# Attention scores of a head pair in two groups of 512 columns instead of three of 384, 384 and 288

## The chip, the cores and the metric

The kernel runs on one core of a Trainium2 chip. The core has a matrix engine (TensorE, "PE" in the profile, with its weight loads as "PEld"), a vector engine (VectorE, "DVE"), a scalar engine (ScalarE, "ACT"), a general engine (GpSimd, "POOL"), and a sync engine (SyncE, "SP") whose queue issues most of the transfers. TensorE writes its results into PSUM, a small memory of eight banks of 512 f32 columns by 128 partitions; the other operands lie in SBUF. The metric is the device time of one execution in microseconds, lower is better.

## What is computed

For 8 batches and 8 heads there are 512 local tokens and 32 global ones, head size 64. Global queries see all keys. A local query sees the 32 global keys and the local keys at most 32 positions away. The attention's output is the input of a dense layer with a softplus between two products.

```python
s_g = scale * np.matmul(q_g, k_all.transpose(0, 1, 3, 2))
out_g = np.matmul(sm(s_g), v_all)
mask = np.abs(pos[:, None] - pos[None, :]) <= window      # window = 32
s_ll = np.where(mask, scale * np.matmul(q_l, k_l.transpose(0, 1, 3, 2)), -1000000000.0)
s_lg = scale * np.matmul(q_l, k_g.transpose(0, 1, 3, 2))
out_l = np.matmul(sm(np.concatenate([s_lg, s_ll], axis=-1)), v_all)
x = np.concatenate([out_g, out_l], axis=2)    # to 4608 rows of 512
h = x @ w_in                                  # 512 x 2048
out = (np.maximum(h, 0.0) + np.log1p(np.exp(-np.abs(h)))) @ w_out
```

## The kernel before

The 64 heads are handled as 32 pairs m, four to a batch; the two heads of a pair lie in partitions 0 to 63 and 64 to 127, so that their products with 64 contraction rows can run side by side on TensorE.

**The local stage.** Pairs 0 to 5 (`M0 = 6`) are computed first, in another form (`scores0`, `turn0`, `values0` and their global counterparts), as 15 steps of a software pipeline with index k; `stage(k, f)` runs phase f of step k. Their exponentials sit in tiles of tags "x", "wo8" and "wo9" (`exps0`). The first 16 weight tiles are split into high and low halves in between.

**The MoE.** For each batch b and each of 16 slices f of the hidden size, `hpart` makes 12 products into tile h, `act` runs softplus (three operations on ACT, one on DVE that writes e, a cast gh on ACT, a difference gl on POOL), and `opart` makes 12 products into the four output tiles o. The operands are f32 numbers split into two reduced-precision halves, three products for each. An o run stands two h runs and one o run or more behind the h run it uses (`behind = 2`), and at a batch's start less (`behind = 1`). A ninth block handles the global tokens. Batch 0 runs while the rest of the weights are still being split (`weights`), batch b needs the pairs 4b to 4b+3 (`split_x`).

**The pieces.** Pairs 6 to 31 are cut into pieces with a position each, and the loop over the MoE's items issues a piece when the position is reached: pair m has its three groups of scores at 12m, 12m+4 and 12m+8, its totals at 12m+18 (`TOT`), its values and normalising at 12m+22 (`VAL`). A batch is 48 positions long. Pieces below `START = 77` are issued inside the local stage, at k = n-2: the first two groups of pair 6.

**A pair.** Global keys are repeated in front of each of six chunks of 96 local keys, so a chunk has 128 keys, held in the partitions. A group p of scores holds two chunks: the queries that can see them, 192 columns a chunk (96 for the last). `scores` (from line 296) makes a product for each chunk and head, f32, into one tile of two PSUM banks, a head to a bank. For pairs 6 and 7 (`m < MPE`) TensorE also adds the mask by a product with the identity, and ACT copies the result; for later pairs DVE adds the mask while it copies (L325). Then DVE takes block maxima over 32 columns with a transposing reduction (L326). After the third group `maxima` folds these (POOL copies L339, small DVE operations L342 to L352), and `probs`, for each group, spreads the maxima (DVE transposes, L360), subtracts them on POOL (L365 to L368), takes the exponential on ACT (L369) and reduces sums on DVE (L374). `totals` folds the sums, `values` multiplies by V, two heads in the two column halves, into a tile of two PSUM banks, and `normalise` scales and writes x.

**Queues and buffers.** The order on TensorE is the order of the program (`mm`); on the other engines a scheduler orders the work, with some orders fixed by hand (`keep`, `after`). In the local stage and early batch 0 scores use the PSUM tiles "oA" and "oB"; with the first o run these banks are given to the output tiles (`output_banks`), and scores and values then share one tile "a" of two banks. The tiles of scores s are four buffers of 2x384 and two of 2x288, the spread maxima mb two of 2x288. The three raw tiles of a pair (queries and keys of a group) are loaded by SP, each right after the group of the pair before that used its buffer.

Of the kernel before, what the change touches and what calls it, by code (L numbers as in the profile page):

```python
# [8 lines left out]
F32 = mybir.dt.float32  # L9
F32R = mybir.dt.float32r  # L10
BF16 = mybir.dt.bfloat16
I32 = mybir.dt.int32
AF = mybir.ActivationFunctionType
ALU = mybir.AluOpType
# [5 lines left out]
P = 128  # L20
NEG = -8.0e9
LOW = -3.0e38
KW = 96
NPC = 3
QW = (288, 288, 192)
KWID = (256, 256, 256)
EW = (0, 544, 1088)
OUT = (0, 512, 736)
NF = DFF // P

M0 = 6
MPE = 8
VAL = 22
TOT = 18
STEP = 3
GW = 75
W_AHEAD = 13
W_PRE = 16
START = 77
RATE = 3  # L40
A_LO = 8
A_UP = 5
# [7 lines left out]
def windows(ap2d, start, stride, count, width):  # L50
    base = ap2d[:, start:start + width]
    return bass.AP(base.tensor, base.offset, [list(base.ap[0]), [stride, count], [1, width]])
# [3 lines left out]
def moe_over_global_local_attention(  # L56
# [11 lines left out]
    nc = tc.nc  # L68
    PSUM = bass.MemoryType.PSUM
    const = ctx.enter_context(tc.tile_pool(name="const", bufs=1))  # L70
    pl = ctx.enter_context(tc.tile_pool(name="pl", bufs=2))
    ps_h = ctx.enter_context(tc.tile_pool(name="ps_h", bufs=2, space=PSUM))
    ps_a = ctx.enter_context(tc.tile_pool(name="ps_a", bufs=1, space=PSUM))
# [3 lines left out]
    ps_s = first_scores.__enter__()  # L77
# [4 lines left out]


    identf = pl.tile([P, P], F32, tag="e", name="identf", bufs=2)
    mask = const.tile([P, 384], BF16, name="mask")
    mask5 = const.tile([P, 96], BF16, name="mask5")
    ident = const.tile([P, P], BF16, name="ident")

    mask0 = pl.tile([P, 2, 2, 224], BF16, tag="rb", name="mask0", bufs=1)
# [2 lines left out]
    for o, w, base, sign in ((32, 32, 0, 1), (64, 32, -96, -1), (96, 128, 32, 1), (96, 128, 32, -1)):  # L92
        r = mask0[:, 0, 1, o:o + w]
# [5 lines left out]
    make_identity(nc, identf)  # L99

    def key_masks():
        nc.vector.memset(mask, 0.0)
        nc.vector.memset(mask5, 0.0)
        for m, o, w, x0, rows in ((mask, 0, 160, 0, P), (mask, 192, 64, 0, P), (mask, 288, 96, 64, P), (mask5, 0, 64, 0, 64)):
            r = m[0:rows, o:o + w]
            nc.gpsimd.affine_select(r, r, pattern=[[1, w]], compare_op=ALU.is_ge, fill=NEG, base=32 + x0, channel_multiplier=-1)
            nc.gpsimd.affine_select(r, r, pattern=[[-1, w]], compare_op=ALU.is_ge, fill=NEG, base=32 - x0, channel_multiplier=1)
        nc.vector.memset(mask[0:32], 0.0)
        for o in (0, 128, 160, 192, 256, 352):
            nc.vector.memset(mask[0:32, o:o + 32], NEG)  # L110

        nc.vector.memset(mask5[0:32], 0.0)
        nc.vector.memset(mask5[0:32, 0:32], NEG)

        nc.vector.memset(mask5[64:128], NEG)

    order = {}

# [7 lines left out]
    def mm(*a, **k):  # L126
        order["pe"] = after(nc.tensor.matmul(*a, **k), "pe").ins  # L127
# [3 lines left out]
    st = {}  # L131
# [28 lines left out]
    count0 = []  # L160

    def exps0(shape, name):
        count0.append(name)
        tag = ("x", "wo8", "x", "wo9")[len(count0) % 4]
        return pl.tile(shape, F32, tag=tag, name=f"e0_{name}", bufs=2 if tag == "x" else 1)

    def soft0(name, ps, views, outs):

# [116 lines left out]
    def load(m, p):  # L285
        w = QW[p] + KWID[p]
        raw = pl.tile([P, 544], F32, tag="raw", name=f"raw{m}_{p}", bufs=3)
        order["load"] = nc.sync.dma_start(out=raw[:, :w], in_=qk[m - M0, :, EW[p]:EW[p] + w]).ins
        st["raw", m, p] = raw
# [3 lines left out]
        nc.sync.dma_start(out=t.rearrange("p h c d -> p (h c d)"), in_=v[m - M0])  # L293
        st["v", m] = t

    def scores(m, p):
        raw = st.pop(("raw", m, p))
        q = QW[p]
        if "o" not in banks:
            ps = ps_s.tile([P, 2, 512], F32, tag=("oA", "oB")[(3 * m + p) % 2], name=f"s_ps{m}_{p}")  # L300
        else:
            ps = ps_a.tile([P, 2, 512], F32, tag="a", name=f"s_ps{m}_{p}")
        parts = ((0, 0, 192), (192, 96, 192 if p < 2 else 96))
        pe_mask = m < MPE
        masks = (mask[:, 0:192], mask[:, 192:384] if p < 2 else mask5)
        for i, (o, qs, w) in enumerate(parts):
            ks = q + 128 * i
            for h in range(2):
                r = slice(64 * h, 64 * h + 64)
                mm(ps[:, h, o:o + w], lhsT=raw[r, ks:ks + P], rhs=raw[r, qs:qs + w],  # L310
                   start=True, stop=not pe_mask, skip_group_check=True)
            for h in range(2 if pe_mask else 0):
                mm(ps[:, h, o:o + w], lhsT=ident, rhs=masks[i], start=False, stop=True, skip_group_check=True)
        if p == 0:
            st["mt", m] = pl.tile([P, 348], F32, tag="mt", name=f"mt{m}", bufs=2)
            nc.gpsimd.memset(windows(st["mt", m], 0, 36, 3, 3), LOW)
        mt = st["mt", m]
        nb = 12 if p < 2 else 9
        s = pl.tile([P, 2, 32 * nb], F32, tag="s" if p < 2 else "s2", name=f"s{m}_{p}", bufs=4 if p < 2 else 2)
        if pe_mask:  # L320
            nc.scalar.copy(s, ps[:, :, 0:32 * nb])  # L321
        else:
            for o, mk in ((0, mask[:, 0:384]),) if p < 2 else ((0, mask[:, 0:192]), (192, mask5)):
                w = mk.shape[1]
                nc.vector.tensor_tensor(s[:, :, o:o + w], ps[:, :, o:o + w], mk.unsqueeze(1).to_broadcast([P, 2, w]), op=ALU.add)  # L325
        order["scores"] = nc.vector.tensor_reduce(windows(mt, 3 + 12 * p, 36, 2, nb), s.rearrange("p h (b k) -> p h b k", k=32),  # L326
                                axis=AX.X, op=ALU.max, apply_transpose=True).ins
        st["s", m, p] = s

    def grid(t, start, *dims):  # L330
        base = t[0:32, start:start + 1]
# [21 lines left out]
        order["maxima"] = i  # L353
        st["e", m] = e

    def probs(m, p):
        s, e = st["s", m, p], st["e", m]
        k = QW[p] // 32
        mb = pl.tile([P, 2, 288], F32, tag="mb", name=f"mb{m}_{p}", bufs=2)
        nc.vector.transpose(mb[:, :, :QW[p]].rearrange("p h (s k) -> p h s k", k=32),  # L360
                            windows(e, 7 * p, 21, 2, k).unsqueeze(3).to_broadcast([P, 2, k, 32]))
        for h in range(2):
            if p < 2:
                sw = s[:, h].rearrange("p (c w) -> p c w", w=192)
                nc.gpsimd.tensor_tensor(sw, sw, windows(mb[:, h], 0, 96, 2, 192), op=ALU.subtract)  # L365
        if p == 2:
            nc.gpsimd.tensor_tensor(s[:, :, 0:192], s[:, :, 0:192], mb[:, :, 0:192], op=ALU.subtract)
            nc.gpsimd.tensor_tensor(s[:, :, 192:288], s[:, :, 192:288], mb[:, :, 96:192], op=ALU.subtract)  # L368
        nc.scalar.activation(s, s, AF.Exp, scale=0.125)  # L369
        if p == 0:  # L370
            st["zt", m] = pl.tile([P, 348], F32, tag="zt", name=f"zt{m}", bufs=2)
            nc.gpsimd.memset(windows(st["zt", m], 0, 36, 3, 3), 0.0)
        nb = 12 if p < 2 else 9
        nc.vector.tensor_reduce(windows(st["zt", m], 3 + 12 * p, 36, 2, nb), s.rearrange("p h (b k) -> p h b k", k=32),  # L374
                                axis=AX.X, op=ALU.add, apply_transpose=True)

    def totals(m):
# [9 lines left out]
    def values(m):  # L387

        vt = st["v", m]
        ps = st["vs", m] = ps_a.tile([P, 2, 512], F32, tag="a", name=f"v_ps{m}")  # L390
        flat = ps.rearrange("p a q -> p (a q)")
        for p in range(NPC):
            s = st.pop(("s", m, p))
            for i, (o, qs, w) in enumerate(((0, 0, 192), (192, 96, 192 if p < 2 else 96))):
                c = OUT[p] + qs
                for h in range(2):
                    mm(flat[64 * h:64 * h + 64, c:c + w], lhsT=vt[:, h, 2 * p + i], rhs=s[:, h, o:o + w],
                       start=p < 2 and i == 0, stop=True, skip_group_check=True)

    SEG = ((lambda t: t[:, 0:128].unsqueeze(1), 0, 1, 128), (lambda t: windows(t, 160, 224, 2, 192), 128, 2, 192))  # L400

# [14 lines left out]
    def pieces():  # L416
        def piece(*fs):
            def go():
                for f in fs:
                    f()  # L420
            return go
        ps = []
        for m in range(M0, M):
            for p in range(NPC):
                fs = [lambda m=m, p=p: scores(m, p)]
                if m + 1 < M:
                    fs.append(lambda m=m, p=p: load(m + 1, p))
                if p == 2:
                    fs.append(lambda m=m: maxima(m))
                    fs += [lambda m=m, q=q: probs(m, q) for q in range(NPC)]  # L430
                ps.append((12 * m + 4 * p, piece(*fs)))
            ps.append((12 * m + TOT, lambda m=m: totals(m)))
            fs = [lambda m=m: values(m), lambda m=m: normalise(m)]
            if m + 2 < M:
                fs.append(lambda m=m: load_v(m + 2))
            ps.append((12 * m + VAL, piece(*fs)))
        ps.sort(key=lambda t: t[0])
        return ps
# [168 lines left out]
    i = order_w.index(("wi", NF - 1))  # L607
# [33 lines left out]
    n = len(steps)  # L641
# [6 lines left out]
    for k in range(-2, n + 2):  # L648
# [9 lines left out]
        if held:  # L658
            r = bits_w(*held)
# [91 lines left out]
```

## Time and profile before

| | |
|---|---|
| median of 3 runs | 1005.15 us (1004.91 to 1005.45) |
| profiled execution, own time | 1005.01 us |
| its span, first to last instruction | 1003.2 us |
| mean granted TensorE clock | 0.987 |
| share of the chain that ended last | TensorE 79%, DVE 1%, all others under 1% |

The profile shows one execution. Its busy shares are averages over stages with different limits, so the stages are read one by one. Ends of matmuls are modelled and overlap their successors, so TensorE's pace is read from start to start. An f32 product appears as two weight loads and two matmuls. All matmuls carry the line of the helper `mm` (L127) and are told apart by tile: h and o for the MoE, s_ps for scores, v_ps for values of pairs 6 to 31, s, s0g, t, t0g, o0g for the local stage.

### The profile page before, as it was taken

How to read it: one execution, taken by the hardware profiler on the slowest of the kernel's cores; microseconds unless marked ns; L12 is line 12 of the kernel's file. 1: busy time of each engine (PE TensorE's matmuls, PEld its weight loads, DVE VectorE, ACT ScalarE, POOL GpSimd, SP SyncE). 2: the span in 40 equal slices, each digit the busy share in tenths (PEclk: the TensorE clock that was granted, in tenths of full speed). 3: DMA queues.
4: the chain of work that ended last, by engine and by line, in shares of the span. 5: the costliest groups of instructions: out<-in, count | busy, mean ns of one | idle time of the engine just before them, and what ended most of it. 6: DMA issues, size and time to landing. Idle time of an engine off the chain costs nothing.

```text
span 1003.2 us, 14264 instructions
## 1 busy us (share of the span) xinstructions
PE 966.0 (96%) x5151; PEld 755.1 (75%) x5151; DVE 645.8 (64%) x1348; ACT 517.5 (52%) x918; POOL 446.1 (44%) x603
## 2 busy tenths in 40 slices
PE   6798989899999999999999999999999999999996
PEld 4576767677777777777777777777777778888895
DVE  6885979856678766776667677776677665211210
ACT  5787656544445544454454444554445445444452
POOL 5664776524444444453345444444435344222221
PEclk9999989989999999999999999999999999999998
DMA  9824322211112111121112111211112100100000
GB/s 354 310 74 144 112 83 60 58 63 48 40 49 90 49 37 48 49 85 43 47 34 90 40 49 49 70 58 49 48 39 89 47 2 16 50 1 1 22 22 21
DMA packets 34302, 66.19 MB, mean 66 GB/s; under 512 B 7608, under 2 KB 11448, under 8 KB 34232
## 3 DMA queue, kind: packets, MB, share of 16 engines
q1 hardware_dynamic: 33416, 65.19, 20.4%
q8 instruction: 40, 0.66, 0.3%
q14 instruction: 30, 0.25, 0.1%
q10 hardware_dynamic: 816, 0.10, 0.1%
HBM read 55.84 MB, written 9.44 MB: 65 GB/s over the span
## 4 chain that ended last, share of the span: by engine, by line
PE 79%; DVE 1%; POOL 0%; issue 0%; ACT 0%; DVEq 0%; POOLq 0%
PE o L127 35%; PE h L127 34%; PE s_ps L127 5%; PE v_ps L127 5%; DVE xl L454 1%; DVE zt L374 0%; POOL wo L499 0%; DVE mb L360 0%; POOL gl L548 0%; DVE wbitswo L490 0%; DVE e L544 0%; ACT ot L566 0%; DVE wlastwo L493 0%; DVE mt L352 0%; DVE mt L342 0%
## 5 line engine op out<-in xcount | busy, mean ns | idle before, releaser
L127 PE MATMUL o<-wo,gh 128*128 128x512 f32 x1088 | 347.5, 400 | 6.2 <-ACT gh L547 4.9
L127 PE MATMUL h<-xh,wi 128*128 128x512 f32 (+1 forms) x1152 | 351.1, 388 | 1.2 <-DVE e L544 0.7
L548 POOL TENSOR_TENSOR gl<-e,gh 128x512 fp32r<-128x512 f32 x136 | 177.8, 1307 | 333.2 <-ACT gh L547 271.1
L127 PEld LDWEIGHTS h<-xh,wi 128*128 128x128 f32 x1152 | 210.3, 190 | 51.4 <-issue 5.6
L127 PEld LDWEIGHTS o<-wo,gh 128*128 128x128 f32 x1088 | 200.9, 189 | 58.3 <-ACT gh L547 5.8
L544 DVE SCALAR_TENSOR_TENSOR e<-h,e 128x512 f32<-128x512 f32 x136 | 93.0, 684 | 234.4 <-ACT e L543 213.9
L127 PE MATMUL h<-xl,wi 128*128 128x512 f32 (+1 forms) x576 | 220.5, 383 | 0.0
L127 PE MATMUL o<-wo,gl 128*128 128x512 f32 x544 | 216.2, 397 | 2.5 <-POOL gl L548 2.5
L541 ACT ACTIVATE e<-h 128x512 f32<-128x512 f32 x136 | 81.3, 598 | 232.2 <-PE h L127 232.2
L547 ACT CAST gh<-e 128x512 fp32r<-128x512 f32 x136 | 84.3, 620 | 112.6 <-DVE e L544 112.6
L365 POOL TENSOR_TENSOR s<-s,mb 128x384 f32<-128x384 f32 x104 | 107.0, 1060 | 51.1 <-DVE mb L360 51.1
L127 PEld LDWEIGHTS h<-xl,wi 128*128 128x128 f32 x576 | 109.0, 189 | 22.7
L127 PEld LDWEIGHTS o<-wo,gl 128*128 128x128 f32 x544 | 102.9, 189 | 27.1 <-POOL gl L548 3.3
L543 ACT ACTIVATE e<-e,one 128x512 f32<-128x512 f32 x136 | 98.4, 723 | 4.2
L542 ACT ACTIVATE e<-e 128x512 f32<-128x512 f32 x136 | 85.7, 630 | 3.4
L325 DVE TENSOR_TENSOR s<-s_ps,mask 128x768 f32<-128x768 f32 (+1 forms) x96 | 64.7, 695 | 29.4 <-PE s_ps L127 29.4
L369 ACT ACTIVATE s<-s 128x768 f32<-128x768 f32 (+1 forms) x78 | 61.7, 790 | 37.1 <-POOL s L365 34.7
L374 DVE TRANSPOSE_TENSOR_REDUCE zt<-s 128x24 f32<-128x768 f32 (+1 forms) x78 | 69.9, 902 | 6.3 <-ACT s L369 4.7
L326 DVE TRANSPOSE_TENSOR_REDUCE mt<-s 128x24 f32<-128x768 f32 (+1 forms) x78 | 69.3, 888 | 5.8 <-ACT s L321 5.1
L127 PEld LDWEIGHTS s_ps<-raw 64*128 64x128 f32 x624 | 48.7, 186 | 29.6 <-issue 22.1
L127 PE MATMUL s_ps<-raw 64*128 64x192 f32 (+1 forms) x624 | 70.1, 340 | 0.7 <-ACT e_g L174 0.7
L127 PEld LDWEIGHTS v_ps<-s,v 128*64 128x64 f32 x624 | 42.5, 137 | 14.3 <-issue 9.0
(134 smaller groups left out, 881.9 us busy)
## 6 DMA issues: line engine op xcount, KB each, us to landing
raw<-in_qk SPq DMA_DIRECT2D x52, 272.0 KB, 2.7
v<-in_v SPq DMA_DIRECT2D x26, 384.0 KB, 3.1
out<-ot SPq DMA_DIRECT2D x34, 256.0 KB, 2.1
wiraw<-in_w_in SPq DMA_DIRECT2D x16, 512.0 KB, 9.1
woraw<-in_w_out SPq DMA_DIRECT2D x16, 512.0 KB, 8.6
raw<-in_qk SPq DMA_DIRECT2D x26, 224.0 KB, 2.5
v<-in_v SPq DMA_DIRECT2D x6, 512.0 KB, 6.0
raw<-in_qk SPq DMA_DIRECT2D x6, 416.0 KB, 7.8
```

What stands on the lines that cost most here:

```text
L127: order["pe"] = after(nc.tensor.matmul(*a, **k), "pe").ins
L325: nc.vector.tensor_tensor(s[:, :, o:o + w], ps[:, :, o:o + w], mk.unsqueeze(1).to_broadcast([P, 2, w]), op=ALU.add)
L326: order["scores"] = nc.vector.tensor_reduce(windows(mt, 3 + 12 * p, 36, 2, nb), s.rearrange("p h (b k) -> p h b k", k=32), axis=AX.X, op=A ...
L365: nc.gpsimd.tensor_tensor(sw, sw, windows(mb[:, h], 0, 96, 2, 192), op=ALU.subtract)
L369: nc.scalar.activation(s, s, AF.Exp, scale=0.125)
L374: nc.vector.tensor_reduce(windows(st["zt", m], 3 + 12 * p, 36, 2, nb), s.rearrange("p h (b k) -> p h b k", k=32), axis=AX.X, op=ALU.add, a ...
L541: nc.scalar.activation(e, ph, AF.Abs)
L542: nc.scalar.activation(e, e, AF.Exp, scale=-1.0)
L543: nc.scalar.activation(e, e, AF.Ln, bias=one)
L544: nc.vector.scalar_tensor_tensor(e, ph, 0.0, e, op0=ALU.max, op1=ALU.add)
L547: nc.scalar.copy(gh, e)
L548: nc.gpsimd.tensor_tensor(gl, e, gh.bitcast(F32), op=ALU.subtract)
```

## The change

A pair's scores, 1056 columns a head before, become 1024 in one order of columns, cut into two groups of 512, a full PSUM bank for each head. Seven products a head take the place of six: the first chunk's product is 160 wide instead of 192 (32 columns of padding are left out), and the third chunk's is made in two parts, 160 columns in the first group and 32 in the second. One mask of 1024 columns takes the place of two masks; for pairs 6 and 7 its product comes first, 512 columns at once, and the scores are accumulated on it. Pairs from 8 on have one mask add a group. One tile of scores s of 2x1024 holds a pair (two buffers). Maxima, exponentials and sums go by the two groups. The spread maxima take four transposes instead of three, into tiles of 2x416, and the subtractions five operations instead of six. `values` has still six products a head, read from the new column order, the first 160 wide. The groups stand at 12m and 12m+6, `TOT` is 17, `VAL` 21 and `START` 80: both groups of pair 6 come before the MoE. The raw tiles are loaded one after the first group and two after the second. The exponentials of the local stage use the tag "s".

```diff
-OUT = (0, 512, 736)
+CHUNKS = ((0, 0, 32, 160), (1, 160, 96, 192), (2, 352, 0, 160), (2, 512, 160, 32), (3, 544, 96, 192), (4, 736, 0, 192), (5, 928, 96, 96))
+VALUES = ((0, 0, 32, 160), (1, 160, 96, 192), (2, 352, 512, 192), (3, 544, 608, 192), (4, 736, 736, 192), (5, 928, 832, 96))
-VAL = 22
-TOT = 18
+VAL = 21
+TOT = 17
-START = 77
+START = 80
...
-    mask = const.tile([P, 384], BF16, name="mask")
-    mask5 = const.tile([P, 96], BF16, name="mask5")
+    mask = const.tile([P, 1024], BF16, name="mask")
...
+        for o, q, w in ((0, 384, 160), (160, 544, 192), (736, 352, 192)):
+            nc.gpsimd.tensor_copy(mask[:, o:o + w], mask[:, q:q + w])
...
-        tag = ("x", "wo8", "x", "wo9")[len(count0) % 4]
+        tag = ("s", "wo8", "s", "wo9")[len(count0) % 4]
...
-    def scores(m, p):
+    def scores(m, g):
...
+        cut = slice(512 * g, 512 * g + 512)
+        for h in range(2 if pe_mask else 0):
+            mm(ps[:, h], lhsT=ident, rhs=mask[:, cut], start=True, stop=False, skip_group_check=True)
+        for c, o, qs, w in CHUNKS:
+            if not cut.start <= o < cut.stop:
+                continue
+            raw, ks, o = st["raw", m, c // 2], QW[c // 2] + 128 * (c % 2), o - cut.start
             for h in range(2):
                 r = slice(64 * h, 64 * h + 64)
                 mm(ps[:, h, o:o + w], lhsT=raw[r, ks:ks + P], rhs=raw[r, qs:qs + w],
-                   start=True, stop=not pe_mask, skip_group_check=True)
-            for h in range(2 if pe_mask else 0):
-                mm(ps[:, h, o:o + w], lhsT=ident, rhs=masks[i], start=False, stop=True, skip_group_check=True)
+                   start=not pe_mask, stop=True, skip_group_check=True)
...
+            st["s", m] = pl.tile([P, 2, 1024], F32, tag="s", name=f"s{m}", bufs=2)
+        s = st["s", m][:, :, cut]
         if pe_mask:
-            nc.scalar.copy(s, ps[:, :, 0:32 * nb])
+            nc.scalar.copy(s, ps)
         else:
+            nc.vector.tensor_tensor(s, ps, mask[:, cut].unsqueeze(1).to_broadcast([P, 2, 512]), op=ALU.add)
...
+    def probs(m, g):
+        s, e = st["s", m], st["e", m]
+        mb = pl.tile([P, 2, 416], F32, tag="mb", name=f"mb{m}_{g}", bufs=2)
+        for o, k, n in (((0, 1, 8), (256, 7, 5)), ((0, 10, 6), (192, 14, 6)))[g]:
+            nc.vector.transpose(mb[:, :, o:o + 32 * n].rearrange("p h (s k) -> p h s k", k=32),
+                                windows(e, k, 21, 2, n).unsqueeze(3).to_broadcast([P, 2, n, 32]))
+        for o, q, w in (((0, 0, 160), (160, 64, 352)), ((512, 64, 32), (544, 0, 384), (928, 288, 96)))[g]:
+            nc.gpsimd.tensor_tensor(s[:, :, o:o + w], s[:, :, o:o + w], mb[:, :, q:q + w], op=ALU.subtract)
+        s = s[:, :, 512 * g:512 * g + 512]
         nc.scalar.activation(s, s, AF.Exp, scale=0.125)
...
+        for k, o, c, w in VALUES:
+            for h in range(2):
+                mm(flat[64 * h:64 * h + 64, c:c + w], lhsT=vt[:, h, k], rhs=s[:, h, o:o + w],
+                   start=k % 2 == 0 and k < 4, stop=True, skip_group_check=True)
...
-            for p in range(NPC):
-                fs = [lambda m=m, p=p: scores(m, p)]
+            for g in range(2):
+                fs = [lambda m=m, g=g: scores(m, g)]
                 if m + 1 < M:
-                    fs.append(lambda m=m, p=p: load(m + 1, p))
+                    fs += [lambda m=m, p=p: load(m + 1, p) for p in ((0,), (1, 2))[g]]
...
-                ps.append((12 * m + 4 * p, piece(*fs)))
+                ps.append((12 * m + 6 * g, piece(*fs)))
```

## What I expected, and why

> **What bounds the kernel now.** I read four views in this order: the page's busy table, the chain of work that ended last, the waits of TensorE, and the windows by stage. The page first:
>
> ```profile
> span 1003.2 us, 14264 instructions
> PE 966.0 (96%) x5151; PEld 755.1 (75%) x5151; DVE 645.8 (64%) x1348; ACT 517.5 (52%) x918; POOL 446.1 (44%) x603
> ```
>
> TensorE is busy nearly throughout, but busy time of pipelined matmuls overlaps, so the chain has to confirm it. Here is the chain over one stretch of the middle; columns are start, length, engine, tile, instructions.
>
> ```profile
> 448.75 0.85 PE s_ps L127 x8
> 449.60 1.59 PE h L127 x6
> 451.19 2.80 PE o L127 x12
> ...
> 466.19 0.72 PE s_ps L127 x8
> 466.90 2.99 PE h L127 x12
> 469.90 1.94 PE v_ps L127 x24
> 471.84 2.96 PE o L127 x12
> ```
>
> Everything here is TensorE. An undisturbed run of 12 MoE matmuls takes 2.80 us; the run after an attention block takes 2.96 to 2.99, so each block costs about 0.17 behind it besides its own length. Now the waits of TensorE from 120 to 205 us (total us, times, longest):
>
> ```profile
> PE o L127 <- ACT gh L547: 4.9, 2, 3.3
> PE o L127 <- POOL gl L548: 2.5, 2, 1.8
> ```
>
> And the windows (length; busy us and instructions of PE, PEld, DVE, ACT, POOL; granted clock; DMA):
>
> ```profile
> 120.00:150.00 30.00, 26.21 (x126) 19.00 (x126) 23.33 (x41) 17.61 (x30) 22.54 (x18) 0.89 0.22 70
> 180.00:200.00 20.00, 17.02 (x96) 12.78 (x94) 17.73 (x35) 11.76 (x21) 12.32 (x17) 1.00 0.26 73
> 200.00:225.00 25.00, 23.61 (x108) 18.00 (x110) 12.60 (x32) 10.22 (x18) 7.06 (x9) 0.86 0.18 63
> ...
> 334.90:444.40 109.50, 109.50 (x578) 84.96 (x577) 78.91 (x175) 53.57 (x87) 49.67 (x72) 1.00 0.19 54
> ```
>
> Three stages follow. First the local stage runs, paced by exchanges between DVE, ACT and TensorE. Then, to about 225 us, the MoE of batch 0 runs beside weight splitting and pairs 6 to 9; TensorE idles 30−26.21 = 3.8, 20−17.02 = 3.0 and 25−23.61 = 1.4 us in the three windows, and the granted clock drops after the idling: about 0.11×26.2 = 2.9 and 0.14×23.6 = 3.3 us more. So batch 0 loses about 14 us. From 225 on every window up to 960 us is like the last row: TensorE never idles, so there a saved us of TensorE is a saved us of the kernel.
>
> **The change in that third stage: pairs 10 to 31, 22 of them.** Their masks are added on DVE, so TensorE has only f32 products, each issued as two passes, the two heads side by side. I need a price per pass and column, and one for a pass too short to hide its weight load. The s0g products give both (start, length, count; a row's pace is read from the start of the next row):
>
> ```profile
> 69.36 1.03 PE L127 MATMUL s0g<-raw 128*128 128x256 f32 x4
> 70.22 0.53 PE L127 MATMUL s0g<-raw,raw 128*128 128x32 f32 x4
> 70.68 0.44 PE L127 MATMUL o<-p_0gh,v 128*64 128x128 f32 x4
> ```
>
> Four 256-column passes take 70.22−69.36 = 0.86, so 0.215 each or 0.84 ns a column: 192, 160 and 96 columns cost 0.161, 0.134 and 0.081 us. Four 32-column passes take 0.46, 0.115 each, where the columns alone would be 0.027; the rest I read as the weight load of 128 columns, which a short pass can't cover.
>
> Now each block. Before: a group of 384 has four steps of 192, 4×0.161 = 0.645, but holds the chain 0.85, plus 0.17 behind it: the switch into and out of a block costs 0.205+0.17 = 0.375. The group of 288 costs 0.72+0.17 = 0.89, so scores cost 2×1.02+0.89 = 2.93 a pair. After: the first group (160, 192, 160) has 2×(0.134+0.161+0.134) = 0.858, with one switch 1.23. The second (32, 192, 192, 96) is the old 288 group plus one 192 product and the 32: 0.89+2×0.161+2×0.115 = 1.44. Together 2.67, so −0.26. One switch fewer gives −0.375, while the columns give +0.12, because the two passes of 32 cost more than the 32 columns that are dropped. Values keep 12 products, and one shrinks from 192 to 160: −2×0.027 = −0.054. A pair gains 0.31 us, and 22 pairs **6.8 us**. Pairs 8 and 9, of the same form, lie in batch 0: **0.6**.
>
> The 32-column price was seen for full 128 rows, not for two 64-row products side by side. Its ends are 0.027 (loads hidden, pair gains 0.49) and 0.23 (the two loads one after the other, pair gains 0.08): 10.8 and 1.8 us over 22 pairs. I take 0.115, the nearest row. The Trainium skill, "TensorEngine Tiling (Array Packing)", section Instruction Overhead, puts the floor of a small matmul at about 60 cycles; by it (an estimate, 25 ns a pass at its 2.4 GHz) the sum would be near the upper end. The row is over four times that floor, so the measurement decides.
>
> **Pairs 6 and 7**, whose mask TensorE adds. Rows around pair 6's first two groups, its third, and one group of pair 7:
>
> ```profile
> 73.54 0.59 PE L127 MATMUL s_ps<-raw 64*128 64x192 f32 x4 [0.74 <-ACT e_g L174]
> ...
> 76.72 0.44 PE L127 MATMUL o<-p_1gh,v 128*64 128x128 f32 x4
> ...
> 96.23 0.40 PE L127 MATMUL h<-xl,wi 128*128 128x512 f32 x1
> ...
> 98.93 0.50 PE L127 MATMUL o<-wo,gh 128*128 128x512 f32 x1 [0.93 <-ACT s L321]
> ...
> 109.90 0.39 PE L127 MATMUL h<-xl,wi 128*128 128x512 f32 x1
> ...
> 111.67 0.48 PE L127 MATMUL o<-wo,gh 128*128 128x512 f32 x1
> ```
>
> A MoE matmul takes 2.80/12 = 0.233. A masked 384 group costs 111.67−109.90−0.233 = 1.54; the 288 group loses half a 192 product (0.16) and half its mask passes (about 0.08): 1.30. Pair 7: 4.4 us before. After, four 512-column bf16 mask passes (0.215 each by the column price above, halved for one pass a cycle: 512×0.42 ns) make 0.86, plus the f32 groups' 2.67: 3.5. **−0.9.** Pair 6 pays 76.72−73.54 = 3.2 for two groups inside the local stage, and 98.93−96.23−0.23 = 2.47 for the third between MoE matmuls, 0.93 of that waiting for ACT's copy, as the output banks lie over the score banks. START 80 puts both new groups into the local stage: 3.5−3.2 = 0.3 more there, 2.47 gone here: **−2.2**. SP issues pair 7's three loads there too instead of two; I cost that at nothing, since pair 7's first scores stand 30 us later, at 110.
>
> **Other engines.** Rows by form (busy us, mean ns):
>
> ```profile
> L326 DVE TRANSPOSE_TENSOR_REDUCE mt<-s 128x24 f32<-128x768 f32 x52 | 49.1, 944 | 0.0
> L326 DVE TRANSPOSE_TENSOR_REDUCE mt<-s 128x18 f32<-128x576 f32 x26 | 20.2, 776 | 5.8 <-ACT s L321 5.1
> L360 DVE STREAM_TRANSPOSE mb<-mt 128x384 f32<-128x384 f32 x26 | 14.9, 574 | 0.0
> L369 ACT ACTIVATE s<-s 128x768 f32<-128x768 f32 x52 | 44.0, 847 | 34.7 <-POOL s L365 34.7
> ```
>
> And POOL's run of one pair in the middle, with a gl between:
>
> ```profile
> 472.14 3.97 POOL L365 TENSOR_TENSOR s<-s,mb 128x384 f32<-128x384 f32 x4 [2.62 <-DVE mb L360]
> 476.07 1.27 POOL L548 TENSOR_TENSOR gl<-e,gh 128x512 fp32r<-128x512 f32 x1
> 477.31 1.01 POOL L367 TENSOR_TENSOR s<-s,mb 128x384 f32<-128x384 f32 x1
> 478.29 0.59 POOL L368 TENSOR_TENSOR s<-s,mb 128x192 f32<-128x192 f32 x1
> ```
>
> A reduction costs 0.88 ns an element plus 0.27: two of 1024 take 2.3 to 2.4 instead of 2×0.944+0.776 = 2.66, for maxima and sums alike. The transposes go from three to four for nearly the same elements (1600, were 1536), which costs less than one whole transpose of 384, 0.57. The mask adds shrink from four instructions to two. So DVE's sum hardly moves. POOL: 2.2 ns a column plus 0.17: five subtractions over 2048 columns take 5.3 instead of 5.57, but the longest takes 1.85 instead of 1.0. All of this is hidden under TensorE after 225 and costs nothing there.
>
> What could move is batch 0. Pair 6's maxima, shifts and sums (2.4 us of reductions, four transposes and the small operations of the maxima on DVE, 5.3 us on POOL) start in the local stage instead of behind 98 us, so they leave the crowded stretch in which TensorE waits for gh and gl. Likewise pair 8's second group stands at 102 of the order instead of 104 and pair 7's values at 105 instead of 106: the end of batch 0 is less crowded. Of the 14 us lost I take 6 as regained, between 0 and 14, and worse than 0 if a third stall appears (7 us, half of 14). Against that, pair 6's DVE and ACT work now stands among the last steps of the local stage and may hold them up: between 0 and 4, I take 1.5.
>
> **Sum.** −6.8−0.6−0.9−2.2−6+1.5 = −15.0. The profiled execution took 1005.0 (1003.2 of span and 1.8 around), the median of the runs is 1005.15: **990**.
>
> **Rivals.** (1) Batch 0 gives all back: it is DVE and POOL, not TensorE, that pace it, and its TensorE gains turn into longer waits. For it: DVE is busy 23.3 of 30 us in the worst window; against: DVE and POOL get less to do there. Then only the 22 pairs count: 1005−6.8 = 998. (2) Batch 0's stalls vanish wholly: 1005−10.5−14 = 981. (3) The change doesn't do what it says for TensorE: the cost of a block goes with its passes, not with the switch. Then a pair is +0.12−0.054 = +0.07 and pairs 6 and 7 alone gain about 3: 1003 to 1005, no change. Against it: equal passes, 12 MoE matmuls, cost 0.17 more only right behind a block. (4) Slower: the shared tile of scores ties the groups together. If POOL may not shift the second group until ACT and DVE are done with the first, POOL stands still for an exponential (847 ns by 1024/768: 1.1) and a reduction (1.2) between 2.6 and 2.75 us of subtractions: 7.7 us in which a gl queued behind waits, where one row now holds it 3.97. One row shows a neighbour of this, with DVE's 32x21 copies held while POOL splits weights:
>
> ```profile
> 130.10 3.67 DVE L383 COPY zt<-zt 32x21 f32<-32x21 f32 x3
> ```
>
> In the middle the 3.7 us more are covered: the gl done at 477.34 is that of the h run of 466.90, whose o run comes after two more o and two more h runs, so after 471.84+2.96+3×2.80 = 483, and 5.8 us are spare. In batch 0, where TensorE waits for gl already, they aren't; two further stalls of 7 us there give 1005−10.4+14 = 1009. It decides once the hold grows by more than what is spare. The Trainium skill, "SBUF — State Buffer", section Who interferes with whom, makes a GpSimd operation hold the port pair it shares with VectorE for the whole instruction, so longer subtractions would push this way; the 3.67 us row fits it.
>
> **Chances.** Forecast (984 to 996) 0.62, (1) 0.24, (2) 0.06, (3) 0.04, (4) 0.04. The range 981 to 1001 leaves out (3), (4) and half of (2). A measurement of this kernel tells 0.2%, 2 us, from no change; so faster 0.92, same 0.04, slower 0.04.
>
> **What would show it.** After 225: two s_ps blocks a pair, 1.06 (0.858+0.205) and 1.27 (1.44−0.17) in the chain, values 1.89, each followed by a run of 2.96 to 2.99; a batch of four pairs 1.2 us shorter than 109.5; no wait of TensorE. The second group's first two passes 0.11 apart. Batch 0: first o run nearer 96 than 98.93 and less than 8.2 us of idle TensorE in the three windows. Wrong if TensorE waits for gl after 225, if the 32-column passes cost twice the load, or if the local stage ends more than 4 us late.

## The result and the profile after

The changed kernel is **slower by 0.8%**: 1012.75 us median (1010.09 to 1014.01, 4 runs) against 1005.03 us, ratio 1.0076 with a 95% interval of [1.0057, 1.0096]. I had forecast 990 us. The page of the changed kernel, busy time and the granted clock in 40 slices:

```profile
span 1011.1 us, 14314 instructions
PE 959.0 (95%) x5236; PEld 763.0 (75%) x5239; DVE 627.2 (62%) x1272; ACT 510.6 (51%) x890; POOL 432.8 (43%) x580
...
PEclk9897899999999999999999999999999999999998
DMA  9824042111111211121112111221112100100000
```

TensorE, DVE, ACT and POOL all have less to do than before (DVE by 18.6 us, although I had expected its sum hardly to move), and still the span is 7.9 us longer. The slices say where to look: in the fourth and fifth slice (76 to 126 us) the clock drops, and in the fifth the DMA engines stand idle.

A ledger by stages locates it. MoE work is the same in both kernels, so I take the first MoE matmul and, for each batch, the start of the first ACT operation that reads h (us, from the trace):

| | before | after | difference |
|---|---|---|---|
| first MoE matmul | 86.14 | 100.36 | +14.2 |
| from there to ACT's first read of batch 0 | 4.66 | 7.14 | +2.5 |
| batch 0 | 118.38 | 114.61 | −3.8 |
| batches 1 to 6, together | 652.82 | 647.72 | −5.1 |
| of these, batches 2 to 5, each | 109.47 | 108.72 | −0.75 |
| batch 7, global tokens, end | 141.23 | 141.29 | +0.1 |

So the steady batches became shorter, as forecast, and the loss arose before the MoE began; batch 0 didn't make up for it. The second row is hardly a loss of TensorE: it makes its second h run in that time, while ACT comes to the first only at 107.50 (below). The chain of the changed kernel in the middle (start, length, engine, tile, instructions) shows the steady part:

```profile
440.64 5.70 PE h L124 x24
446.34 1.27 PE s_ps L124 x16
447.61 2.94 PE o L124 x12
...
453.30 1.89 PE v_ps L124 x24
455.19 2.99 PE o L124 x12
...
460.94 1.07 PE s_ps L124 x12
462.01 3.00 PE o L124 x12
```

Two score blocks a pair of 1.07 and 1.27 us and values of 1.89, each with a MoE run of 2.94 to 3.00 behind it: the forecast had 1.06, 1.27, 1.89 and 2.96 to 2.99.

The loss is in the timeline of TensorE, first of the kernel before, then of the changed one (in brackets the idle time before, and what ended it):

```profile
82.83 1.10 PE L127 MATMUL o0g<-p0g2gh,v 128*128 128x64 f32 x8 [1.02 <-ACT p0g2gh L262]
...
86.14 1.22 PE L127 MATMUL h<-xh,wi 128*128 128x512 f32 x2 [0.45 <-ACT xa L232]
```

```profile
91.11 1.97 PE L124 MATMUL o0g<-p0g2gh,v 128*128 128x64 f32 x8 [8.84 <-ACT p0g2gh L259]
...
100.36 1.22 PE L124 MATMUL h<-xh,wi 128*128 128x512 f32 x2 [4.15 <-ACT xa L229]
...
113.41 1.22 PE L124 MATMUL h<-xh,wi 128*128 128x512 f32 x2 [5.61 <-DVE e L529]
```

TensorE stands for 8.8 us before the last step of the local stage (1.0 before the change), for 4.2 before the first MoE matmul (0.45) and for 5.6 soon after. Each time it waits for an eviction or for softplus, ordinary work that has become late. ACT's timeline shows what came before it, first of the kernel before, then of the changed one:

```profile
81.38 0.67 ACT L481 ACTIVATE wbitswi<-wiraw 128x512 f32<-128x512 f32 x1
81.96 0.34 ACT L232 COPY xa<-o 128x256 f32<-128x256 f32 x1
82.21 0.57 ACT L262 COPY p0g2gh<-t0g 128x512 f32<-128x512 f32 x1
```

```profile
81.31 0.68 ACT L483 CAST wo<-woraw 128x512 fp32r<-128x512 f32 x1 [0.90 <-DVE woraw L478]
84.57 0.66 ACT L466 ACTIVATE wbitswi<-wiraw 128x512 f32<-128x512 f32 x1 [2.58 <-DMA wiraw<-in_w_in]
87.21 0.67 ACT L466 ACTIVATE wbitswo<-woraw 128x512 f32<-128x512 f32 x1 [1.98 <-DMA woraw<-in_w_out]
88.71 1.06 ACT L357 ACTIVATE s<-s 128x1024 f32<-128x1024 f32 x1 [0.83 <-POOL s L355]
89.67 0.65 ACT L466 ACTIVATE wbitswi<-wiraw 128x512 f32<-128x512 f32 x1
90.23 0.34 ACT L229 COPY xa<-o 128x256 f32<-128x256 f32 x1
90.48 0.58 ACT L259 COPY p0g2gh<-t0g 128x512 f32<-128x512 f32 x1
...
107.50 0.60 ACT L526 ACTIVATE e<-h 128x512 f32<-128x512 f32 x1
```

The eviction p0g2gh, for which TensorE waits, has moved from 82.21 to 90.48. Before, one weight operation stands ahead of it; now there are two that wait for transfers, then pair 6's exponential, which waits for POOL's subtractions, and only then the same weight operation. Whether it is this order that holds the eviction up is for the experiments; in e5 below it changes back.

### The profile page after: what moved, and what is told of

Same layout as the page of the kernel before. It is cut to its first block, busy times and chain, and to the rows that moved or that the text cites. A ratio compares the mean times of both kernels' runs of the same rounds, so it can differ in the third digit from the quotient of the medians.

```text
span 1011.1 us, 14314 instructions
## 1 busy us (share of the span) xinstructions
PE 959.0 (95%) x5236; PEld 763.0 (75%) x5239; DVE 627.2 (62%) x1272; ACT 510.6 (51%) x890; POOL 432.8 (43%) x580
## 4 chain that ended last, share of the span: by engine, by line
PE 75%; DVE 13%; POOL 4%; ACT 4%; issue 3%; POOLq 0%; ACTq 0%; DVEq 0%
PE h L124 34%; PE o L124 32%; PE s_ps L124 4%; PE v_ps L124 4%; POOL s L355 2%; DVE wbitswo L475 1%; ACT e L171 1%; DVE wiraw L478 1%; DVE mt L319 1%; DVE xl L439 1%; DVE wbitswi L475 1%; DVE woraw L478 1%; DVE sums L168 1%; DVE e L529 1%; POOL gl L533 1%
## 5 line engine op out<-in xcount | busy, mean ns | idle before, releaser
L124 PEld LDWEIGHTS h<-xh,wi 128*128 128x128 f32 x1152 | 214.3, 191 | 61.9 <-DVE e L529 12.3
L355 POOL TENSOR_TENSOR s<-s,mb 128x320 f32<-128x320 f32 (+4 forms) x130 | 137.3, 1092 | 69.4 <-DVE mb L352 69.4
L361 DVE TRANSPOSE_TENSOR_REDUCE zt<-s 128x32 f32<-128x1024 f32 x52 | 64.6, 1241 | 37.4 <-ACT s L357 37.4
L357 ACT ACTIVATE s<-s 128x1024 f32<-128x1024 f32 x52 | 55.0, 1059 | 33.8 <-POOL mt L312 28.4
L124 PEld LDWEIGHTS s_ps<-raw 64*128 64x128 f32 x728 | 53.9, 186 | 19.1 <-issue 19.1
L319 DVE TRANSPOSE_TENSOR_REDUCE mt<-s 128x32 f32<-128x1024 f32 x52 | 64.1, 1233 | 5.6 <-ACT s L316 5.0
L124 PE MATMUL s_ps<-raw 64*128 64x192 f32 (+3 forms) x728 | 64.4, 313 | 0.3
L318 DVE TENSOR_TENSOR s<-s_ps,mask 128x1024 f32<-128x1024 f32 x48 | 57.7, 1201 | 5.0 <-PE s_ps L124 5.0
L352 DVE STREAM_TRANSPOSE mb<-mt 128x512 f32<-128x512 f32 (+1 forms) x104 | 52.6, 563 | 0.9
```

The source lines that it names most:

```text
L318: nc.vector.tensor_tensor(s, ps, mask[:, cut].unsqueeze(1).to_broadcast([P, 2, 512]), op=ALU.add)
L319: order["scores"] = nc.vector.tensor_reduce(windows(st["mt", m], 4 + 16 * g, 36, 2, 16), s.rearrange("p h (b k) -> p h b k", k=32), axis=A ...
L355: nc.gpsimd.tensor_tensor(s[:, :, o:o + w], s[:, :, o:o + w], mb[:, :, q:q + w], op=ALU.subtract)
L361: nc.vector.tensor_reduce(windows(st["zt", m], 4 + 16 * g, 36, 2, 16), s.rearrange("p h (b k) -> p h b k", k=32), axis=AX.X, op=ALU.add, a ...
```

## The experiments

Theory A: pair 6's second half (maxima, shifts, exponentials), issued inside the local stage at START 80, holds up the last weight splits and evictions. Theory B: the weight loads come late, because raw loads stand ahead of them on SP. Theory C: the new shapes or tags slow the local stage whatever START is.

**e1: START 75 alone.**

```diff
-START = 80
+START = 75
```

> The changed kernel with START 75 instead of 80: only the first group of pair 6 is issued inside the local stage; its second group, maxima and shifts come in batch 0, about where the third group stood in the kernel before. Theory A (pair 6's maxima, shifts and exponentials stand in the in-order queues of DVE, ACT and POOL ahead of the last weight splits and evictions of the local stage, and hold it up): the first MoE matmul moves from 100.4 back to 86 to 88 us, the 5 us won after batch 0 stay, total 996 to 1001. Theory B (the three raw loads ahead of the weight loads on SP make the weights late): also 86 to 89, since only one raw load is issued there. Theory C (the wider operations or the new tag of the local stage's exponentials slow the local stage whatever START is): first MoE matmul stays above 95, total 1007 or more.

Measured: 1001.44 us, ratio 0.9967 [0.9954, 0.998]. First MoE matmul 88.52, batch 0 116.99, batches 2 to 5 108.71 each. The total is 0.4 above the range of theory A. With this one number changed the new groups are 0.3% faster than the kernel before, and C falls. (The old groups weren't run with START 75, so this isn't the shape alone.) START costs some 11 us (1012.75 in the first comparison, 1001.44 here, each with the kernel before at 1005); it sets both the place of pair 6's second half and the pace of the pieces in batch 0, which e11 separates.

**e2: the old groups, but all three of pair 6 in the local stage.**

```diff
-START = 77
+START = 81
-        while k >= n - 2 and pcs[0][0] < min(12 * M0 + 8 * (k - n + 3), START):
+        while k >= n - 2 and pcs[0][0] < min(12 * M0 + 9 * (k - n + 3), START):
```

> The kernel before, with START 81 and the bound of the local stage's loop raised, so that its third group of pair 6 with maxima and shifts is issued inside the local stage, as the change does. Theory A: the first MoE matmul moves from 86.1 to 96 to 101 us, batch 0 wins some 4 us back, total 1010 to 1016. Theory B: the same delay, since the third raw load moves too (e3 tells A from B). Theory C: 86 to 90, total 1003 to 1006.

Measured: 1022.03 us, ratio 1.0166 [1.0151, 1.0181]. First MoE matmul at 100.54, as in the changed kernel, behind the same wait:

```profile
93.60 1.97 PE L127 MATMUL o0g<-p0g2gh,v 128*128 128x64 f32 x8 [7.25 <-ACT p0g2gh L262]
...
100.54 0.79 PE L127 MATMUL h<-xh,wi 128*128 128x512 f32 x1 [1.84 <-ACT xa L232]
```

So the old kernel, without one of the new shapes, becomes 17 us slower by the move (START 81 quickens the pieces of batch 0 too, but the first MoE matmul is late already). Batch 0 won back only 0.9 us (117.44 against 118.38), not the 4 that I had expected, so the total lies above my range.

**e3: both score groups of pair 6 early, its maxima and shifts at 12m+9.**

```diff
+                late = [lambda m=m: maxima(m)] + [lambda m=m, q=q: probs(m, q) for q in range(2)]
-                if g:
-                    fs.append(lambda m=m: maxima(m))
-                    fs += [lambda m=m, q=q: probs(m, q) for q in range(2)]
+                if g and m > M0:
+                    fs += late
                 ps.append((12 * m + 6 * g, piece(*fs)))
+                if g and m == M0:
+                    ps.append((12 * m + 9, piece(*late)))
```

> The changed kernel with START 80 kept: both groups of scores of pair 6 and all three raw loads of pair 7 stay in the local stage, but pair 6's maxima and shifts (with exponentials and sums) become a piece of their own at position 12m+9, in early batch 0. Theory A: first MoE matmul at 86 to 90, total 994 to 1001. Theory B: first MoE matmul still at 95 or later, total 1006 or more. Theory C: the same as B.

Measured: 1004.42 us, ratio 0.9994 [0.9984, 1.0003]; first MoE matmul 88.64. The local stage recovers with the scores and all three raw loads still in it, so A holds for the local stage and B doesn't explain it. But the total is above A's range: batch 0 takes 120.70, more than the 114.6 of the changed kernel and the 117.0 of e1. The pace of its pieces is still that of START 80; e11, with the same pace, takes 121.13.

**e5: weight bits with buffers of their own.** In the local stage the tiles of weight bits (`wbits`, written by the ACT operation L466) and the spread maxima share the tag mb, two buffers. In the code pair 6's two spread-maxima tiles come just ahead of the bits of the weight tile wi8, and the evictions xa and p0g2gh are ordered by hand behind wi8's ACT operation.

```diff
-            a = pl.tile([P, 512], I32, tag="mb", name=f"wbits{kind}{k}", bufs=2)
+            a = pl.tile([P, 512], I32, tag="wb", name=f"wbits{kind}{k}", bufs=2)
```

> The changed kernel, START 80 kept, with the tiles of weight bits that shared the tag mb with the spread maxima given two buffers of their own. Theory A1 (the delay of the local stage comes through the two mb buffers: pair 6's two spread-maxima tiles stand in the rotation ahead of the bits of weight wi8, whose ACT operation must wait until POOL has subtracted, and the last evictions of the local stage are ordered behind it): the first MoE matmul comes at 86 to 91 us, total 996 to 1004. Theory A2 (it is the plain work of pair 6 in the queues of DVE, ACT and POOL): still at 96 or later, total 1008 or more.

Measured: 1010.89 us, ratio 1.0053 [1.0036, 1.0069]. Both theories are right in part. The first MoE matmul is back at 88.01 us, so the 12 us before it did come through the two shared buffers. ACT's timeline shows how: the eviction p0g2gh again follows wi8's operation at once, and the operation that waits for a transfer now stands behind it.

```profile
81.33 0.68 ACT L466 ACTIVATE wbitswi<-wiraw 128x512 f32<-128x512 f32 x1
...
82.16 0.60 ACT L259 COPY p0g2gh<-t0g 128x512 f32<-128x512 f32 x1
...
84.66 0.68 ACT L466 ACTIVATE wbitswi<-wiraw 128x512 f32<-128x512 f32 x1 [1.77 <-DMA wiraw<-in_w_in]
```

But batch 0 now takes 126.90 instead of 114.61, and batch 1 begins at 220.0 instead of 222.1: TensorE waits twelve matmuls later instead. Timelines of TensorE, POOL and DVE in this run:

```profile
88.01 1.22 PE L124 MATMUL h<-xh,wi 128*128 128x512 f32 x2 [2.35 <-ACT xa L229]
...
98.95 1.22 PE L124 MATMUL h<-xh,wi 128*128 128x512 f32 x2 [5.86 <-ACT yg L276]
```

```profile
88.47 6.12 POOL L355 TENSOR_TENSOR s<-s,mb 128x320 f32<-128x320 f32 x5
```

```profile
86.36 0.42 DVE L473 TENSOR_SCALAR wbitswi<-wbitswi 128x512 int32<-128x512 int32 x1
...
89.81 1.91 DVE L473 TENSOR_SCALAR wbitswi<-wbitswi 128x512 int32<-128x512 int32 x1
91.64 2.50 DVE L473 TENSOR_SCALAR wbitswo<-wbitswo 128x512 int32<-128x512 int32 x2
```

POOL subtracts pair 6's maxima for 6.1 us without a break. Beside it DVE's weight operation L473, 0.42 us alone, takes 1.91, and two of them 2.50. The Trainium skill, "SBUF — State Buffer", section Who interferes with whom, says that a VectorE operation in a two-port mode and a GpSimd operation exclude each other for a whole instruction; these durations agree with it. So does the kernel before: the nine of its L473 operations (L488 there) with no POOL operation beside them take 0.43 us at most, the others up to 1.50, and one that starts at 82.08 beside a POOL operation ending at 82.84 ends at 83.12. No run shows which mode the operation is in, and that the port is the cause was not tried by itself.

**e6: as e5, raw loads only after the second group.**

```diff
-                    fs += [lambda m=m, p=p: load(m + 1, p) for p in ((0,), (1, 2))[g]]
+                    fs += [lambda m=m, p=p: load(m + 1, p) for p in ((), (0, 1, 2))[g]]
```

> As e5, and the three raw loads of a pair are all issued after the second group of the pair before, none after the first. In the changed kernel SP's queue stands from 81.6 to 123.7 us behind the raw load of pair 8, which waits for pair 7's first group, with four weight loads behind it. If late weights are part of what batch 0 loses, batch 0 takes 2 to 5 us less than in e5; if not, it takes the same within 1 us. The batches from 1 on stay at 108.7.

Measured: 1008.79 us, ratio 1.0038 [1.0023, 1.0052]; batch 0 takes 123.88, 3.0 less than in e5. SP's timeline, first of e5, then of e6:

```profile
78.62 2.52 SPq L452 DMA_DIRECT2D woraw<-in_w_out  x2
119.25 0.33 SPq L285 DMA_DIRECT2D raw<-in_qk  x1
119.63 0.94 SPq L452 DMA_DIRECT2D wiraw<-in_w_in  x2
```

```profile
80.31 4.55 SPq L452 DMA_DIRECT2D woraw<-in_w_out  x3
85.93 9.88 SPq L452 DMA_DIRECT2D wiraw<-in_w_in  x2
117.82 0.34 SPq L285 DMA_DIRECT2D raw<-in_qk  x1
```

With a raw load of pair 8 next in the queue, SP issues nothing for 38 us (81.14 to 119.25; 42 in the changed kernel, 17 in the kernel before) and the weight loads behind it wait too; without it they go out by 96. This is a smaller loss, 3.0 us of batch 0 in this arrangement; the medians differ by 2.1, and the intervals of the two ratios overlap.

**e8 and e9: the same two edits on e1.**

> As e1 (START 75), with the weight bits' own buffers of e5. Theory A1 says the shared mb buffers hold up the weight split wherever pair 6 to 9 stand beside it: batch 0 takes 2 to 5 us less than the 117.0 of e1, total 996 to 999. The plain-work theory A2 says the order of the work, not its buffers, decides: batch 0 within 1 us of e1 or longer, as the split runs further ahead of the softplus work on DVE; total 1000 to 1004.

> As e1 (START 75), with all three raw loads issued after the second group, as in e6. If weight loads waiting on SP behind raw loads are part of what batch 0 loses here too, batch 0 takes 1 to 4 us less than 117.0 and the total is 997 to 1000; if not, 1001 as e1.

Measured: e8 1003.71 us, ratio 0.9983 [0.997, 0.9996]; e9 1001.13, 0.9961 [0.9948, 0.9975]. Both start the MoE 2.3 us earlier (86.14 and 86.23), and both give it back or more: batch 0 takes 121.89 and 118.88. With START 75 neither is a cost of its own. The times are those that A2 had forecast; that the weight split runs ahead of the softplus work in e8 was not shown.

**e11: pair 6's second half out of the local stage, pieces of batch 0 paced as in the changed kernel.**

```diff
-        while k >= n - 2 and pcs[0][0] < min(12 * M0 + 8 * (k - n + 3), START):
+        while k >= n - 2 and pcs[0][0] < min(12 * M0 + 8 * (k - n + 3), 75):
```

> The changed kernel with the local stage's bound at 75, as in e1, but the pace of the pieces in batch 0 still counted from 80, so pair 6's second group, maxima and shifts follow the first MoE item and pairs 7 to 9 stand as in the changed kernel. If only the place of pair 6's second half matters, the first MoE matmul stays at 88 to 89 and the total at 999 to 1003, as e1. If the earlier pieces of pairs 7 to 9 matter as well, batch 0 takes 3 us or more above 117.0, near the 120.7 of e3, and the total is 1003 to 1007.

Measured: 1006.4 us median (1002.81 to 1007.08), ratio 1.0004 [0.9994, 1.0014]; batch 0 takes 121.13, e1 116.99. START has a second effect: counted from 80, the pieces of pairs 6 to 9 come earlier in batch 0, beside the weight split, and that costs about 4 us there. Of the 11 us between the changed kernel and e1, the place of pair 6's second half is 6.3 (1012.75 to 1006.4) and the pace 5.0 (1006.4 to 1001.44).

**e4, e7, e10: where the pieces stand against the batches.** In the changed kernel TensorE waits once a batch for gl. POOL's, ACT's and TensorE's timelines at such a place:

```profile
319.98 5.24 POOL L355 TENSOR_TENSOR s<-s,mb 128x320 f32<-128x320 f32 x5 [3.57 <-DVE mb L352]
325.17 0.10 POOL L312 MEMSET mt<- 128x12 f32 x1
325.23 1.28 POOL L533 TENSOR_TENSOR gl<-e,gh 128x512 fp32r<-128x512 f32 x1
```

```profile
322.22 0.62 ACT L532 CAST gh<-e 128x512 fp32r<-128x512 f32 x1 [0.43 <-DVE e L529]
322.75 1.06 ACT L357 ACTIVATE s<-s 128x1024 f32<-128x1024 f32 x1
```

```profile
326.57 0.50 PE L124 MATMUL o<-wo,gl 128*128 128x512 f32 x1 [0.21 <-POOL gl L533]
```

The gh is done at 322.84, but its gl must wait for five subtractions, 5.24 us in one run, until 325.23. The matmul before it starts about 0.6 instead of 0.23 us earlier, so 0.37 us a batch go. The kernel before has no such wait. I tried to move the pieces away from this place. e4 and e7 differ from e1 in `VAL = 22, TOT = 18`, and in `STEP = 4` with the buffers of e5; e10 in `STEP = 2`.

> As e1, and VAL 22 and TOT 18 as in the kernel before, so that the first group of a pair no longer falls on the last item of a batch. In the changed kernel TensorE waits at each end of a batch about 0.37 us for gl, whose lead over its use there is 0.1 us instead of 3.1. If the place of the group is the cause, the wait goes: batches 1 to 5 take 108.35 instead of 108.72 us, total about 2 us below e1. If it is the longer DVE operations, nothing changes against e1.

> As e1 (START 75) with the buffers of e5 and STEP 4 instead of 3, which moves all pieces one position earlier against the batches and keeps their distances. If the shared mb buffers also hold up weight splitting in batch 0, batch 0 takes 2 to 5 us less than the 117.0 of e1; if not, the same. If the place of a pair's first group on the last item of a batch makes TensorE wait for gl, batches 1 to 5 take 108.3 to 108.4 instead of 108.7. Total 994 to 1000.

> As e1 with STEP 2, all pieces one position later against the batches, so that a pair's first group falls behind the batch's first h items instead of on its last item. e4 and e7 moved pieces earlier and lost 3 to 4 us a batch. If the wait of 0.37 us at each batch's end comes from the first group on the last item, batches 1 to 5 take 108.3 to 108.4 and the total is 2 us below e1; if the values and x of the next batch come too late, the batches take 110 or more and the total is 1010 or more.

Measured: e4 1013.74 us, ratio 1.0082 [1.0065, 1.01], batches 110.3 to 111.9; e7 1022.87, 1.0178 [1.0161, 1.0195], batches 111.6 to 113.2 and batch 0 120.29; e10 1001.54, 0.9957 [0.9942, 0.9972], batches 108.08. The longest waits of TensorE that differ, in e4 and in e7:

```profile
PE s_ps L124 <- issue: 10.5, 5, 2.1
```

```profile
PE o L124 <- ACT gh L532: 9.5, 6, 3.3
...
PE s_ps L124 <- issue: 5.0, 5, 1.0
```

In e4 the values stand two positions ahead of the next scores instead of three, and scores wait 2.1 us at each end of a batch; I read this as the shared PSUM tile not being free, which the profile doesn't name. The distance alone can't be the reason: in the kernel before it is two as well, and scores don't wait. In e7 the softplus at a batch's end is late instead. My expectation that an earlier place gains fails in both. The guess on which it rested, that the wait for gl comes from the group on the last item, isn't refuted: from 225 us on that wait is gone in e4, stays in e7 and is gone in e10. In e10 the pieces come one position later, and the gl goes ahead of the subtractions:

```profile
312.82 1.28 POOL L533 TENSOR_TENSOR gl<-e,gh 128x512 fp32r<-128x512 f32 x1 [2.27 <-issue]
314.05 5.54 POOL L355 TENSOR_TENSOR s<-s,mb 128x320 f32<-128x320 f32 x5
```

But batch 0 takes 120.87 there, 3.9 more than in e1.

**e12: e10's place for the later batches, e1's pace for batch 0.**

```diff
-START = 80
+START = 75
-STEP = 3
+STEP = 2
-        at = ... START + (first + 48 - START) * gone[b] / total[b]
+        at = ... START + (first + 49 - START) * gone[b] / total[b]
```

> As e1 (START 75), with STEP 2 for the batches from 1 on and the pace of batch 0 kept as in e1 (first + 49 there instead of first + 48). e10 made batches 1 to 5 take 108.08 us instead of 108.71 but gave 3.9 us back in batch 0, where its pieces came late. If the two are independent, batch 0 takes 117.0 us as in e1, the later batches 108.08, and the total is 3 to 4 us below e1, 997 to 998.5. If the end of batch 0 depends on the pieces that now follow it, batch 0 takes 119 or more and the total is 1000 to 1002.

Measured: **998.5 us** (998.33 to 998.79), ratio 0.9938 [0.9924, 0.9951], the fastest version here, 0.6% faster than the kernel before; its range of 997 to 998.5 holds. Batches 2 to 5 take 108.08 to 108.12. The first MoE matmul is at 86.09, batch 0 takes 118.81, not the 117.0 that I had expected; batch 1 begins at 210.42, in e1 at 210.03, so the split between the two stages moved, not their sum.

## Why the prediction was wrong

The span moved by +7.9 us where I had forecast −15.0. Of the 22.9 between them, 12.7 are the end of the local stage (14.2 instead of 1.5), 8.4 are batch 0 from the first MoE matmul on (−1.3 instead of −0.6−0.9−2.2−6 = −9.7) and 1.7 the steady batches (−5.1 instead of −6.8).

**Step that failed: "Against that, pair 6's DVE and ACT work now stands among the last steps of the local stage and may hold them up: between 0 and 4, I take 1.5."** It was 14.2 us; the prediction's own sign, a local stage that ends more than 4 us late, was right. I had listed the amount of work added and given no row for the bounds. What decided was the order of the work: two shared buffers put wi8's weight operation behind POOL's subtractions (e5), and the evictions that TensorE waits for are fixed by hand behind that operation. e2 shows the same loss in the old kernel.

**Second step that failed: "Of the 14 us lost I take 6 as regained."** Nothing was. From the first MoE matmul to batch 1, before and after, in the columns of the prediction's windows:

```profile
86.14:209.17 123.03, 113.58 (x519) 86.20 (x520) 97.86 (x172) 70.44 (x118) 76.23 (x76) 0.93 0.23 72
```

```profile
100.36:222.11 121.75, 109.76 (x510) 86.23 (x513) 85.67 (x141) 66.22 (x109) 62.73 (x61) 0.93 0.22 70
```

TensorE's idle time rose from 123.03−113.58 = 9.45 us to 121.75−109.76 = 11.99, at the same granted clock, although DVE and POOL had less to do. The stretch is 1.3 us shorter only because TensorE's own work in it shrank, by 4.0 at the prices of the forecast: 0.9 for pair 7, 0.6 for pairs 8 and 9, 2.5 for pair 6's third group, which has left it. The stalls moved, the two longest to 107.80 to 113.41 and 178.04 to 182.11. The sign that I had named, less than 8.2 us of idle time in three windows, came true (0.2+2.1+2.1 = 4.4) and misled, because the first of these stalls and half of the second lie outside the windows. In e11, with that pace and without pair 6's second half in the local stage, batch 0 is even 2.8 us longer than before, so less total work for DVE and POOL didn't mean less waiting.

**"I cost that at nothing, since pair 7's first scores stand 30 us later"** looked at the user of the raw loads and not at what queues behind them on SP. The next raw load, pair 8's, held the weight loads for some 40 us; e6 puts 3.0 us of batch 0 on it in that arrangement, and with START 75 (e9) the total didn't change.

**The third stage was right in its prices, but TensorE did wait.** I said 0.31 us a pair and no wait of TensorE. The blocks of scores and values cost what I had said, but TensorE waits for gl at the end of each of five batches, which the prediction had named as a sign of being wrong. So batches 2 to 5 lost 0.75 us for four pairs; with the 0.37 of waiting added that is 1.12, or 0.28 a pair. Where the wait is gone (e10, e12) they lost 109.47−108.08 = 1.39, or 0.35 a pair, with the pieces in another place. The switch price of 0.375 a block carried over. So did the price of a short pass, nearly: in the second group the first two passes start 0.133 us apart and the second and third 0.112 (473.258, 473.391, 473.503), where I had 0.115 from s0g. The Trainium skill, "TensorEngine Tiling (Array Packing)", section Instruction Overhead, has a floor of about 60 cycles, 25 ns by the prediction's estimate; these passes, each with a load of 128 columns of f32 weights, take over four times that.

**The rivals.** (1) that batch 0 gives all back was too mild, as it left the local stage out. (3) falls by the third stage. (4) named the right sign, but not the mechanism: POOL's five subtractions run through without waiting for the first group's exponential (5.24 us from 319.98, while the exponential starts at 322.75), so the shared tile of scores doesn't hold the second group up there. What did come of it is the longer unbroken run ahead of gl, 0.37 us a batch.

**What stays open.** The runs show that the place and pace of the pieces of pairs 6 to 9 cost the 11 us between the changed kernel and e1, and that the shared buffers made the late start of the MoE. But the parts don't add up: free buffers gain 12 us at one point and lose 12 behind it. How much of batch 0's loss is DVE slowed beside POOL wasn't separated, and neither was what the new shape is worth with each at its best place.

## What to carry to other kernels

Price a steady loop by TensorE's own rows and it will hold; price a move of work into a stage that runs on exchanges between engines by what is queued behind it, buffers and hand-made orders included, and not by the amount of work alone. When a change bundles a new shape with a new position, split them before judging: here the new shape at START 75 is 4 us faster than the kernel before, and START 80 alone costs 11. A constant that sets both a place and a pace, as START does, is two changes.

## What I had not expected of the hardware

A VectorE operation of 0.42 us took 1.91 us beside a GpSimd run of 6.1 us. And idle time between MoE matmuls cost twice. After the wait that ended at 113.41, twelve of them took 4.92 us in the chain of the changed kernel instead of 2.80, and after the one that ended at 182.11 they took 4.60. The granted clock was 0.58 in the first of these stretches and back at 1.00 right behind it:

```profile
113.41 4.92 PE h L124 x12
```

```profile
113.40:118.30 4.90, 4.89 (x13) 3.89 (x14) 0.69 (x1) 2.88 (x6) 4.78 (x4) 0.58 0.02 3
118.30:121.10 2.80, 2.80 (x14) 2.31 (x13) 0.14 (x1) 2.39 (x4) 1.07 (x2) 1.00 0.00 0
```

The columns of the last two rows are those of the windows in the prediction. The first MoE matmuls don't differ in this: from the first run of twelve to the next it is 4.18 us before (86.14 to 90.32) and 4.48 after (100.36 to 104.84), slow in both kernels (granted clocks of 0.69 and 0.62). The 2.5 us in the ledger's second row are therefore mostly ACT, which is busy with weight operations until it reads h at 107.50.
